# A second rows buffer, one mask tied behind hand-ordered GpSimd work, and a new hand order with dummy matmuls

## The chip, the cores and the metric

The kernel runs on one core of a Trainium2 chip. The metric is device time in microseconds of a whole execution. Names of engines as in the profile: PE is TensorE (PEld its weight loads), DVE is VectorE, ACT is ScalarE, POOL is GpSimd, and SP is the engine whose queue issues nearly all DMAs. Each engine works through its own queue in order, and waits on semaphores for the others.

## The reference

Three layers, one after the other, in float32:

```python
# 1: scan over chunks of 32 positions: x (4, 8, 768, 32), a (4, 8, 768), B and C (4, 8, 768, 16)
log_a = np.log(np.clip(a, 1e-06, 1.0))
for c in range(nc):
    cum = np.cumsum(la, axis=-1)
    L = np.exp(cum[:, :, :, None] - cum[:, :, None, :]) * causal
    M = np.einsum('bhin,bhjn->bhij', Cc, Bc) * L
    y[:, :, sl] = M @ xc + (Cc @ state) * exp(cum)          # written as einsums
    state = exp(sum(la)) * state + sum_j(Bc x xc * exp(cum[-1] - cum))
# 2: x = y as (3072, 256)
h = x @ w_in                      # (256, 2048)
x = np.maximum(0.01 * h, h) @ w_out
# 3: eight experts; each token goes to one
logits = x @ w_gate + modality_bias[modality_id]
e_idx = np.argmax(logits, axis=1)
gate_w = probs[np.arange(N), e_idx]
for e in range(E):
    out[mask] = gate_w[mask, None] * (np.maximum(x[mask] @ w1[e], 0.0) @ w2[e])
```

## The kernel before, in words

**Tiling.** The scan is done in 24 chunks of 128 positions (0 to 23, six for each batch entry). The 3072 tokens form six blocks of 512, four chunks each. Layer 2 takes a block in 16 steps f of 128 hidden units: `mm1` makes `h` (six matmuls 128x512, since operands are split into a high and a low float32r part), ACT and DVE make `sa`, `gg`, `gh`, `gl` from it, and `mm2` adds to two tiles `y` (six matmuls). So a step is twelve matmuls. Layer 3 takes tiles of 256 tokens of one expert; the token lists (`il`) are built on the chip by `ranks`, the rows of x lie in DRAM (`yx`), and a gather brings them back (`xg`).

**Chunks.** A chunk needs `e`, the exponentials of differences of sums, with a mask. For chunks 0 to 3 the sums come from matmuls (`bc_mm`), ACT makes the exponentials (`bc_exp`), and POOL masks them in two halves of 128x512 (`bc_mask`). For chunks 4 and later the sums are broadcast by a DMA from DRAM (`e<-cumd`, 512 KB each, after `cumd<-cumrow` has been written), POOL masks all 128x1024 at once (`attn_mask`), and ACT makes the exponentials behind that (`attn_exp`). Then DVE multiplies (`cb_mul`), PE sums (`p3_mm`, tile `psy`), and ACT and DVE write the chunk's columns of `xh` and `xl`, from which `mm1` reads.

**Weights of layer 2.** They come as 64-bit numbers, 1 MB at a time (`raw`; four for w_in, four for w_out, three buffers), and each half of 128x512 is turned into a high and a low part in five operations: ACT `hb`, POOL `lb` (about 2 us), DVE two operations (the second writes `hb`), ACT `wih` or `woh`, and the subtraction that writes `wil` or `wol`, also on POOL here. The halves called i0, i1 (w_in, first quarter) and o0, o1 (w_out, first quarter) are done in the prologue.

**What sets the order.** The prologue (chunks 0 to 3 and the halves i0, i1, o0, o1) stands in the list `STAGED`, which four engines keep among these entries. All else is placed by a scheduler that simulates the program: the list `sched` says at which of the 16 steps of a block a piece is offered, and numbers in `Q` shift these slots. `sh1` shifts the chunks of block 1 (4 to 7). An operation that is not in `STAGED` may be placed between entries of `STAGED`. SP's queue is ordered by the same scheduler. A DMA on SP waits, among others, for the one eight places ahead of it.

**Rows buffer.** Per block, `route` writes the reciprocal of the softmax sum into the last column of `ysb`, `rows` writes the block's 512 rows into it in two copies, and `rows_out` sends it to `yx`. Before the change there is one `ysb` of 128x1056 for all six blocks.

All operations that the helper class records carry line 153 in the profile, so rows are told apart by tiles.

Of the kernel before, what the change touches and what calls it, by code (L numbers as in the profile page):

```python
# [8 lines left out]
F32 = mybir.dt.float32  # L9
# [5 lines left out]
ALU = mybir.AluOpType  # L15
# [17 lines left out]
 'xe': 2,  # L33
 'se': 8,
 'me': 7,
 'sh1': -2,
 'sh': 0,
 'ld': 9,
 'cd': 4,
# [49 lines left out]
def kernel(  # L89
# [21 lines left out]
    P = 128  # L111
# [140 lines left out]
    def consts_b():  # L252
# [25 lines left out]
        v.memset(base, 0.0)  # L278
        v.memset(wg, 0.0)
        g.memset(ysb, 0.0)  # L280
        nc.sync.dma_start(out=yx[NT:NT + 1, :], in_=ysb[0:1, 0, :])
        nc.sync.dma_start(out=wg[:, :, 0:NE], in_=w_gate.rearrange("(k p) e -> p k e", p=P))
        nc.sync.dma_start(out=modi, in_=mod.bitcast(I32).rearrange("(c p w) -> p c w", p=P, w=2))
        nc.sync.dma_start(out=mb, in_=mbias.unsqueeze(0).to_broadcast([P, 2, NE]))
# [114 lines left out]

    def bc_mm(c, q):  # L400
        b, cc = divmod(c, NCB)
        bc = psy.tile([P, 512], F32, tag="y", name="bc")
        cs = slice(cc * P, (cc + 1) * P)
        if c:
            t_.matmul(bc, lhsT=cumb[:, cs], rhs=negm[:, 4 * q:4 * q + 4].unsqueeze(2).to_broadcast([96, 4, P]), start=True, stop=False)
        for k in range(4):
            r = b * H + 4 * q + k
            o = bc[:, k * P:(k + 1) * P]
            if c:
                t_.matmul(o, lhsT=id3[:, r:r + 1].to_broadcast([96, P]), rhs=cumb[:, cs], start=False, stop=(k == 3))  # L410
# [268 lines left out]
    def route(j, src):  # L679
# [287 lines left out]
    STAGED = [
        (decay_a,), (tr_mm, 0), (bc_mm, 0, 0), (bc_mm, 0, 1), (decay_b,), (tr_c, 0), (tr_b, 0), (decay_rows,),
        (bc_exp, 0, 0), (bc_mask, 0, 0), (bc_exp, 0, 1), (bc_mask, 0, 1), (cb_mm, 0), (decay_high,), (attn_cd, 1),
        (hb, "i0", 0, 0), (lb, "i0"), (decay_low_s,), (cb_bs, 0), (cb_mul, 0, 0), (cb_mul, 0, 1), (decay_low_v,),  # L970
        (cb_mul, 0, 2), (cb_mul, 0, 3), (decay_out,), (tr_mm, 1), (tr_d, 1), (tr_c, 1), (tr_b, 1), (tr_de, 1),
        (bc_mm, 1, 0), (bc_mm, 1, 1), (bc_exp, 1, 0), (bc_mask, 1, 0), (bc_exp, 1, 1), (bc_mask, 1, 1),
        (p3_mm, 0), (orr, "i0"), (p3_x, 0), (p3_st, 0), (decay_full_mm,), (decay_full,), (hb, "i1", 0, 1), (cast, "i0"),
        (attn_cd, 2), (cb_mm, 1), (cb_bs, 1), (cb_mul, 1, 0), (cb_mul, 1, 1), (cb_mul, 1, 2), (cb_mul, 1, 3), (lb, "i1"),
        (tr_mm, 2), (tr_d, 2), (tr_c, 2), (tr_b, 2), (tr_de, 2), (bc_mm, 2, 0), (bc_mm, 2, 1),
        (bc_exp, 2, 0), (bc_mask, 2, 0), (bc_exp, 2, 1), (bc_mask, 2, 1), (p3_mm, 1), (p3_x, 1), (p3_st, 1), (orr, "i1"),
        (sub, "i0"), (cast, "i1"), (attn_cd, 3), (cb_mm, 2), (cb_bs, 2), (cb_mul, 2, 0), (cb_mul, 2, 1), (cb_mul, 2, 2),
        (cb_mul, 2, 3), (tr_mm, 3), (tr_d, 3), (tr_c, 3), (tr_b, 3), (tr_de, 3), (bc_mm, 3, 0), (bc_mm, 3, 1),
        (bc_exp, 3, 0), (bc_mask, 3, 0), (bc_exp, 3, 1), (bc_mask, 3, 1), (p3_mm, 2), (p3_x, 2), (p3_st, 2),
        (sub, "i1"), (hb, "o0", 0, 0), (lb, "o0"), (hb, "o1", 0, 1), (lb, "o1"),  # L980
        (cb_mm, 3), (cb_bs, 3), (cb_mul, 3, 0), (cb_mul, 3, 1), (cb_mul, 3, 2), (cb_mul, 3, 3), (p3_mm, 3), (p3_x, 3), (p3_st, 3),
        (orr, "o0"), (cast, "o0"), (sub, "o0"), (orr, "o1"), (cast, "o1"), (sub, "o1"),
    ]
# [148 lines left out]
```

## Time and profile before

| | |
|---|---|
| median of 3 runs | 561.11 us (558.36 to 562.27) |
| profiled execution, its own time | 560.4 us |
| its span in the trace | 558.3 us |
| PE busy | 508.1 us (91%) |
| DVE, ACT, POOL busy | 351.8 (63%), 312.8 (56%), 194.9 us (35%) |

The sum of the prediction is made against the profiled execution: 558.3 us of span and 2.1 us around it. In the page's second part each digit is the busy share of one fortieth of the span (14 us) in tenths. In lists of instructions a row has the start, the busy time, engine, line, operation, tiles and count, and in brackets how long the engine was idle before it and what ended that. Slices of the second part and the windows show busy time, not progress: a PE that runs at the lower of its two clock levels is also busy.

### The profile page before, as it was taken

The page shows a single profiled execution, that of the slowest core. Times are in us where ns is not written, and L with a number is a line of the kernel's source. Part 1 is how long each engine was busy: PE and PEld are TensorE (multiplying, and loading weights), DVE is VectorE, ACT ScalarE, POOL GpSimd, SP SyncE. Part 2 cuts the span into 40 slices and gives each one's busy share as a digit, 9 for nine tenths or more (in the row PEclk, how much of TensorE's full clock was granted, in tenths as well). Part 3 has the DMA queues.
Part 4 walks back from the last instruction along what each step waited for, and adds up shares of the span by engine and source line. Part 5 has one row for each costly group of instructions (what it writes and reads, how often), then busy time and mean ns, then how long its engine had stood idle before and what let it go on. Part 6 is the DMA issues. An engine that isn't in the chain of part 4 may idle for free.

```text
span 558.3 us, 9625 instructions
## 1 busy us (share of the span) xinstructions
PE 508.1 (91%) x3491; PEld 413.8 (74%) x3491; DVE 351.8 (63%) x729; ACT 312.8 (56%) x651; POOL 194.9 (35%) x167
## 2 busy tenths in 40 slices
PE   7749887899999999999999999698989999999991
PEld 5426555677776777677767777576879999999991
DVE  4738998866656775766576766436486665555640
ACT  5426857774655665565556546244446666665640
POOL 5448788410311020102110020451054364665431
PEclk9868998999999999999999999899999999999996
DMA  8995652330236123523340075626059966777400
GB/s 199 147 256 119 175 157 53 58 59 9 52 51 148 17 52 54 112 46 58 38 107 1 2 61 116 213 72 92 0 171 79 298 212 190 230 240 237 147 20 23
DMA packets 128311, 61.01 MB, mean 109 GB/s; under 512 B 84545, under 2 KB 120514, under 8 KB 128258
## 3 DMA queue, kind: packets, MB, share of 16 engines
q1 hardware_dynamic: 125186, 53.94, 43.4%
q0 software_dynamic: 3072, 6.41, 3.6%
q8 instruction: 29, 0.48, 0.4%
q14 instruction: 24, 0.20, 0.1%
HBM read 53.73 MB, written 6.60 MB: 108 GB/s over the span
## 4 chain that ended last, share of the span: by engine, by line
PE 65%; DVE 10%; issue 6%; DMA 6%; ACT 5%; SPq 3%; POOL 2%; POOLq 0%; DVEq 0%; ACTq 0%
PE h L153 19%; PE y L153 18%; PE hp L153 11%; PE o L153 10%; DMA il<-ids,pi 3%; PE psy L153 3%; DVE gl L153 2%; DVE hb L153 2%; DVE e L153 2%; ACT e L153 2%; DMA yx<-ysb 1%; PE cb L153 1%; SPq L373 1%; DMA e<-cumd 1%; DVE gg L153 1%
## 5 line engine op out<-in xcount | busy, mean ns | idle before, releaser
L153 ACT CAST gh<-gg 128x512 fp32r<-128x512 f32 x96 | 59.5, 620 | 75.8 <-DVE gg L153 75.5
L153 DVE TENSOR_TENSOR gl<-gg,gh 128x512 fp32r<-128x512 f32 x96 | 73.8, 768 | 30.1 <-ACT gh L153 27.9
L153 POOL TENSOR_SCALAR_AFFINE_SELECT e<-e 128x1024 f32<-128x1024 f32 (+1 forms) x28 | 27.4, 985 | 170.2 <-DMA e<-cumd 107.1
L153 PE MATMUL h<-xh,wih 128*128 128x512 f32 x192 | 80.0, 421 | 5.8 <-DVE gg L153 4.9
L153 PE MATMUL y<-gl,woh 128*128 128x512 f32 x192 | 78.0, 406 | 6.5 <-DVE gl L153 6.4
L153 DVE TENSOR_TENSOR gg<-sa,h 128x512 f32<-128x512 f32 x96 | 65.6, 683 | 28.9 <-ACT sa L153 24.5
L153 PE MATMUL h<-xl,wih 128*128 128x512 f32 x192 | 76.9, 401 | 0.0
L153 PE MATMUL y<-gh,wol 128*128 128x512 f32 x192 | 75.8, 395 | 0.0
L153 PE MATMUL h<-xh,wil 128*128 128x512 f32 x192 | 75.7, 397 | 0.0
L153 ACT ACTIVATE sa<-h 128x512 f32<-128x512 f32 x96 | 57.0, 593 | 32.3 <-PE h L153 29.7
L153 PE MATMUL hp<-x2h,w1s 128*128 128x256 f32 x384 | 71.9, 283 | 0.0
L153 PE MATMUL o<-w2s,hh 128*128 128x256 f32 x384 | 69.3, 285 | 0.0
L153 PE MATMUL y<-gh,woh 128*128 128x512 f32 x192 | 66.5, 406 | 2.4 <-ACT gh L153 2.4
L153 DVE SCALAR_TENSOR_TENSOR hl<-hp,hh 128x512 fp32r<-128x512 f32 x48 | 33.0, 691 | 52.7 <-ACT hh L153 38.3
L153 PEld LDWEIGHTS hp<-x2h,w1s 128*128 128x128 f32 x384 | 61.1, 192 | 0.6
L153 POOL TENSOR_TENSOR w2s<-r,w2s 128x1024 fp32r<-128x1024 f32 x12 | 33.1, 2756 | 73.4 <-ACT w2s L153 51.1
L153 PEld LDWEIGHTS o<-w2s,hh 128*128 128x128 f32 x384 | 58.4, 191 | 0.4 <-issue 0.4
L153 PE MATMUL hp<-x2l,w1s 128*128 128x256 f32 x192 | 53.3, 283 | 0.0
L153 PEld LDWEIGHTS h<-xh,wih 128*128 128x128 f32 x192 | 36.6, 193 | 20.2 <-DVE gg L153 9.3
L153 PE MATMUL o<-w2s,hl 128*128 128x256 f32 x192 | 51.1, 283 | 0.0
L153 ACT ACTIVATE e<-e,ncum 128x128 f32<-128x128 f32 x160 | 51.0, 395 | 0.0
L153 ACT ACTIVATE hh<-hp 128x512 fp32r<-128x512 f32 x48 | 28.5, 597 | 39.9 <-PE hp L153 34.0
(191 smaller groups left out, 919.2 us busy)
## 6 DMA issues: line engine op xcount, KB each, us to landing
r<-in_moe_w_dram SPq DMA_DIRECT2D x48, 512.0 KB
e<-cumd SPq DMA_DIRECT2D x20, 512.0 KB
raw<-in_moe_w_in_dram SPq DMA_DIRECT2D x4, 1024.0 KB
raw<-in_moe_w_out_dram SPq DMA_DIRECT2D x4, 1024.0 KB
yx<-ysb SPq DMA_DIRECT2D x6, 528.0 KB
xt<-in_x_dram SPq DMA_DIRECT2D x24, 128.0 KB
ct<-in_C_dram SPq DMA_DIRECT2D x24, 64.0 KB
bt<-in_B_dram SPq DMA_DIRECT2D x24, 64.0 KB
```

Source lines behind the costliest of these rows:

```text
L153: r = f(*args, **kw)
L373: nc.sync.dma_start(out=xt, in_=x[b, :, sl, :].rearrange("h p d -> p h d"))
```

## The change

`ysb` gets a second half, and block j uses half j % 2; the clearing of it covers both. `consts_b` is emitted before the staged list and not behind it. The mask of chunk 4 gets an order dependency (no semaphore) on the last subtraction of the staged list. `warm(c, n)` puts n matmuls of zeros in front of a chunk's `bc_mm`, into the tile that `bc_mm` then overwrites: six ahead of chunk 1's transposes and four ahead of chunk 2's. In `STAGED` the second DVE step of half i1 (`orr`) and `attn_cd` of chunk 3 move ahead of chunk 1's p3, and half o1 is started later. `sh1` goes from -2 to 1, which offers all work on chunks 4 to 7 three steps later.

```diff
- 'sh1': -2,
+ 'sh1': 1,
...
-    ysb = cst.tile([P, 4, YW], F32, name="ysb")
+    ysb = cst.tile([P, 2, 4, YW], F32, name="ysb")
...
     def attn_mask(c):
         e = ch[c]["e"]
         r = g.affine_select(out=e, in_=e, pattern=[[0, H], [1, P]], compare_op=ALU.is_ge, fill=NEG, base=0, channel_multiplier=-1)
+        if c == NC0:
+            tc.add_manual_dep(
+                r.ins, dk["last"].ins.name, mybir.DependencyInfo(mybir.DependencyClass.NoSync, mybir.DependencyReason.DATA),
+                reason="behind the first chunks and conversions in the queue: it waits for a transfer",
+            )
...
     def bc_mm(c, q):
         b, cc = divmod(c, NCB)
-        bc = psy.tile([P, 512], F32, tag="y", name="bc")
+        bc = ch[c].get(("bc", q))
+        if bc is None:
+            bc = psy.tile([P, 512], F32, tag="y", name="bc")
...
-        v.reciprocal(out=ysb[:, 0:nq, DM:DM + 1], in_=sm.unsqueeze(2))
+        v.reciprocal(out=ysb[:, j % 2, 0:nq, DM:DM + 1], in_=sm.unsqueeze(2))
...
-        readers.append(s.copy(out=ysb[:, 2 * qq:2 * qq + 2, 0:DM], in_=yr.rearrange("p (q d) -> p q d", q=2)))
+        readers.append(s.copy(out=ysb[:, j % 2, 2 * qq:2 * qq + 2, 0:DM], in_=yr.rearrange("p (q d) -> p q d", q=2)))
...
-        nc.sync.dma_start(out=yx[t0:t0 + n, :].rearrange("(q p) d -> p q d", p=P), in_=ysb[:, 0:nq, :])
+        nc.sync.dma_start(out=yx[t0:t0 + n, :].rearrange("(q p) d -> p q d", p=P), in_=ysb[:, j % 2, 0:nq, :])
...
+    consts_b()
     cvs = {}
+
+    def warm(c, n):
+        bc = psy.tile([P, 512], F32, tag="y", name="bc")
+        for _ in range(n):
+            t_.matmul(bc, lhsT=zer[:, 0:P], rhs=zer, start=True, stop=True)
+        ch[c]["bc", 0] = bc
...
     def sub(key):
         (r, hi, lo, eng), c = cvs.pop(key)
-        eng.tensor_tensor(out=lo, in0=c[1] if W64 else r, in1=hi.bitcast(F32), op=ALU.subtract)
+        dk["last"] = eng.tensor_tensor(out=lo, in0=c[1] if W64 else r, in1=hi.bitcast(F32), op=ALU.subtract)
...
-        (cb_mul, 0, 2), (cb_mul, 0, 3), (decay_out,), (tr_mm, 1), (tr_d, 1), (tr_c, 1), (tr_b, 1), (tr_de, 1),
+        (cb_mul, 0, 2), (cb_mul, 0, 3), (decay_out,), (warm, 1, 6), (tr_mm, 1), (tr_d, 1), (tr_c, 1), (tr_b, 1), (tr_de, 1),
...
```

**POOL's queue, from the masks of chunk 2 on.** Before, `e_197` and `e_204` are chunks 2 and 3, `e_585`, `e_603`, `e_720`, `e_750` are chunks 4 to 7, `wil` the subtractions of i0 and i1, and `raw_171` holds o0 and o1:

```order
L153 AFFINE_SELECT e_197<-e_197 128x512 x2
L153 TENSOR_TENSOR wil_138<-hb_286,wih_137 128x512
L153 AFFINE_SELECT e_585<-e_585 128x1024
L153 AFFINE_SELECT e_603<-e_603 128x1024
L153 AFFINE_SELECT e_720<-e_720 128x1024
L153 AFFINE_SELECT e_204<-e_204 128x512 x2
L153 TENSOR_TENSOR wil_138<-hb_354,wih_137 128x512
L153 TENSOR_SCALAR lb_489<-raw_171 128x512
L153 TENSOR_SCALAR lb_493<-raw_171 128x512
L153 AFFINE_SELECT e_750<-e_750 128x1024
L153 TENSOR_SCALAR lb_591<-raw_208 128x512
L153 TENSOR_TENSOR wol_140<-hb_488,woh_139 128x512
```

In the changed kernel, from the masks of chunk 3 (`e_204`) on; chunks 4 to 7 are now `e_595`, `e_613`, `e_680`, `e_862`:

```order
L153 AFFINE_SELECT e_204<-e_204 128x512 x2
L153 TENSOR_TENSOR wil_138<-hb_400,wih_137 128x512
L153 TENSOR_SCALAR lb_526<-raw_171 128x512
L153 TENSOR_SCALAR lb_566<-raw_171 128x512
L153 AFFINE_SELECT e_613<-e_613 128x1024
L153 AFFINE_SELECT e_680<-e_680 128x1024
L153 AFFINE_SELECT e_862<-e_862 128x1024
L153 TENSOR_SCALAR lb_601<-raw_208 128x512
L153 TENSOR_TENSOR wol_140<-hb_525,woh_139 128x512
L153 TENSOR_SCALAR lb_619<-raw_208 128x512
L153 TENSOR_TENSOR wol_140<-hb_565,woh_139 128x512
L153 AFFINE_SELECT e_595<-e_595 128x1024
```

Chunk 3's masks, the subtraction of i1 and both `lb` of `raw_171` no longer stand behind any mask of a DMA'd chunk. The masks of chunks 5, 6 and 7 now stand together ahead of the next `lb` and of both `wol`; chunk 4's, the first that block 1 needs, stands behind all of them.

**SP's queue around the broadcasts.** Before:

```order
L371 DMA ct_602<-in_C_dram 128x8x16
L350 DMA cumd_96<-cumrow_245 32x768
L373 DMA xt_582<-in_x_dram 128x8x32
L372 DMA bt_601<-in_B_dram 128x8x16
L371 DMA ct_719<-in_C_dram 128x8x16
L375 DMA e_585<-cumd_96 128x8x128
L375 DMA e_603<-cumd_96 128x8x128
L373 DMA xt_600<-in_x_dram 128x8x32
L375 DMA e_720<-cumd_96 128x8x128
L375 DMA e_750<-cumd_96 128x8x128
L607 DMA raw_580<-in_moe_w_out_dram 128x4x256
```

In the changed kernel:

```order
L350 DMA cumd_96<-cumrow_272 32x768
L371 DMA ct_612<-in_C_dram 128x8x16
L373 DMA xt_592<-in_x_dram 128x8x32
L372 DMA bt_611<-in_B_dram 128x8x16
L371 DMA ct_679<-in_C_dram 128x8x16
L375 DMA e_595<-cumd_96 128x8x128
L614 DMA raw_590<-in_moe_w_out_dram 128x4x256
L375 DMA e_613<-cumd_96 128x8x128
L375 DMA e_680<-cumd_96 128x8x128
L375 DMA e_862<-cumd_96 128x8x128
L373 DMA xt_610<-in_x_dram 128x8x32
```

The write of the sums goes one DMA earlier, and the 1 MB load of w_out's second quarter now stands between the broadcast of chunk 4 and those of chunks 5 to 7.

**ACT's queue in block 0**, in the changed kernel, from the exponentials of chunk 4 to the first operation on step f = 4 (`sa_834`):

```order
L153 ACTIVATE e_595<-e_595,ncum_122 128x128 x7
L153 CAST wih_137<-hb_618 128x512
L153 ACTIVATE e_595<-e_595,ncum_122 128x128
L153 ACTIVATE e_613<-e_613,ncum_122 128x128 x4
L153 ACTIVATE hb_751<-raw_590 128x512
L153 CAST woh_139<-hb_751 128x512
L153 COPY btt_726<-ps_721 128x128
L153 CAST xh_630<-psy_700 128x2x128
L153 ACTIVATE cdt_729<-ps_721,mask2_106 128x128 x2
L153 ACTIVATE e_613<-e_613,ncum_122 128x128 x4
L153 ACTIVATE hb_759<-raw_590 128x512
L153 ACTIVATE sa_834<-h_827 128x512
```

Before, chunk 4's eight exponentials stood ahead of block 0's very first `sa`; now they, and what follows, stand ahead of the `sa` of its fifth step. From the early steps of block 2 to the end the order on every engine is the same in both kernels but for single neighbours.

## Rows read from the trace of the kernel before

**Rows 1.** The page's second part: PE's busy tenths in 40 slices.

```profile
PE   7749887899999999999999999698989999999991
```

**Rows 2.** The chain that ended last, from 0 to 120 us: start, length, what.

```profile
25.76 7.37 issue
33.13 5.65 DMA e<-cumd
...
44.89 4.17 PE h L153 x12
...
103.57 1.66 PE h L153 x6
```

**Rows 3.** Busy time by windows: PE, PEld, DVE, ACT, POOL, clock, DMA share, GB/s.

```profile
30.00:40.00 10.00, 4.16 (x37) 2.30 (x36) 0.97 (x3) 2.18 (x6) 4.42 (x5) 0.67 1.07 283
...
90.00:100.00 10.00, 10.00 (x46) 7.71 (x45) 9.05 (x14) 5.94 (x12) 8.76 (x6) 0.91 0.01 2
...
120.00:140.00 20.00, 20.00 (x111) 15.67 (x108) 12.26 (x29) 11.67 (x29) 1.09 (x1) 1.00 0.20 40
```

**Rows 4.** POOL's instructions in order of time, 20 to 60 us.

```profile
33.17 1.09 POOL L153 TENSOR_SCALAR_AFFINE_SELECT e<-e 128x1024 f32<-128x1024 f32 x1 [7.41 <-DMA e<-cumd]
35.13 1.09 POOL L153 TENSOR_SCALAR_AFFINE_SELECT e<-e 128x1024 f32<-128x1024 f32 x1 [0.87 <-DMA e<-cumd]
37.77 2.27 POOL L153 TENSOR_SCALAR_AFFINE_SELECT e<-e 128x1024 f32<-128x1024 f32 x3 [1.55 <-DMA e<-cumd]
...
47.63 2.00 POOL L153 TENSOR_SCALAR lb<-raw 128x512 int32<-128x512 uint16 x1 [1.41 <-DVE hb L153]
...
53.00 1.30 POOL L153 TENSOR_TENSOR wol<-hb,woh 128x512 fp32r<-128x512 f32 x1
54.94 2.05 POOL L153 TENSOR_SCALAR lb<-raw 128x512 int32<-128x512 uint16 x1 [0.64 <-DVE hb L153]
...
58.88 2.31 POOL L153 TENSOR_SCALAR lb<-raw 128x512 int32<-128x512 uint16 x1 [0.64 <-DVE hb L153]
```

**Rows 5.** ACT's instructions in order of time: the exponentials of chunk 3.

```profile
30.14 1.10 ACT L153 ACTIVATE e<-bc 128x512 f32<-128x512 f32 x2
```

**Rows 6.** SP's DMA issues in order of time, 0 to 70 us.

```profile
24.54 0.81 SPq L371 DMA_DIRECT2D ct<-in_C_dram  x1
...
27.95 1.19 SPq L375 DMA_DIRECT2D e<-cumd  x2
```

**Rows 7.** Windows of 2 us, columns as in group 3.

```profile
34.00:36.00 2.00, 0.16 (x1) 0.00 (x0) 0.00 (x0) 0.00 (x0) 1.13 (x2) 1.00 1.22 257
...
38.00:40.00 2.00, 0.00 (x0) 0.00 (x0) 0.00 (x0) 0.00 (x0) 2.00 (x3) 0.50 1.00 341
```

**Rows 8.** DVE's instructions in order of time, then the chain from 300 to 420 us.

```profile
354.02 0.18 DVE L153 RECIPROCAL ysb<-sm 128x4 f32<-128x4 f32 x1 [6.09 <-DMA yx<-ysb]
...
347.36 6.57 DMA yx<-ysb
```

**Rows 9.** PE's instructions in order of time, 345 to 384 us.

```profile
349.72 0.61 PE L153 MATMUL y<-gh,woh 128*128 128x512 f32 x2
354.32 0.19 PE L153 MATMUL rp<-ohb,tris 128*128 128x32 bf16 x1 [3.99 <-DVE ohb L153]
...
358.73 0.63 PE L153 MATMUL y<-gh,woh 128*128 128x512 f32 x2
...
361.48 0.61 PE L153 MATMUL y<-gh,woh 128*128 128x512 f32 x2
...
375.55 0.60 PE L153 MATMUL xps<-ident,xg 128*128 128x128 f32 x4
```

**Rows 10.** All engines in order of time, 0 to 60 us.

```profile
2.87 0.97 POOL L153 MEMSET ysb<- 128x1056 f32 x1
...
7.64 0.36 DVE L153 COPY cum<-p 128x192 f32<-128x192 f32 x1 [0.90 <-PE p L153]
...
14.22 0.33 PE L153 MATMUL ps<-ident,ct 128*128 128x128 f32 x1 [1.51 <-DVE e L153]
```

More of the change, by code (lines that the diff above doesn't have):

```diff
@@ L280, in consts_b @@
         g.memset(ysb, 0.0)
-        nc.sync.dma_start(out=yx[NT:NT + 1, :], in_=ysb[0:1, 0, :])
+        nc.sync.dma_start(out=yx[NT:NT + 1, :], in_=ysb[0:1, 0, 0, :])
         nc.sync.dma_start(out=wg[:, :, 0:NE], in_=w_gate.rearrange("(k p) e -> p k e", p=P))
@@ L970 @@
         (hb, "i0", 0, 0), (lb, "i0"), (decay_low_s,), (cb_bs, 0), (cb_mul, 0, 0), (cb_mul, 0, 1), (decay_low_v,),
-        (cb_mul, 0, 2), (cb_mul, 0, 3), (decay_out,), (tr_mm, 1), (tr_d, 1), (tr_c, 1), (tr_b, 1), (tr_de, 1),
+        (cb_mul, 0, 2), (cb_mul, 0, 3), (decay_out,), (warm, 1, 6), (tr_mm, 1), (tr_d, 1), (tr_c, 1), (tr_b, 1), (tr_de, 1),
         (bc_mm, 1, 0), (bc_mm, 1, 1), (bc_exp, 1, 0), (bc_mask, 1, 0), (bc_exp, 1, 1), (bc_mask, 1, 1),
-        (p3_mm, 0), (orr, "i0"), (p3_x, 0), (p3_st, 0), (decay_full_mm,), (decay_full,), (hb, "i1", 0, 1), (cast, "i0"),
@@ L974 @@
[L974 to L982, printed above, removed]
+        (p3_mm, 0), (orr, "i0"), (p3_x, 0), (p3_st, 0), (decay_full_mm,), (decay_full,), (cb_mm, 1), (warm, 2, 4),
@@ new lines @@
+        (hb, "i1", 0, 1), (cast, "i0"), (cb_bs, 1), (cb_mul, 1, 0), (cb_mul, 1, 1), (attn_cd, 2), (cb_mul, 1, 2),
+        (cb_mul, 1, 3), (lb, "i1"), (tr_mm, 2), (tr_d, 2), (tr_c, 2), (tr_b, 2), (tr_de, 2), (orr, "i1"), (attn_cd, 3),
+        (bc_mm, 2, 0), (bc_mm, 2, 1), (bc_exp, 2, 0), (bc_mask, 2, 0), (bc_exp, 2, 1), (bc_mask, 2, 1),
+        (p3_mm, 1), (p3_x, 1), (cast, "i1"), (sub, "i0"), (p3_st, 1), (cb_mm, 2), (cb_bs, 2),
+        (cb_mul, 2, 0), (cb_mul, 2, 1), (cb_mul, 2, 2), (cb_mul, 2, 3), (tr_mm, 3), (tr_d, 3), (tr_c, 3), (tr_b, 3), (tr_de, 3),
@@ L983 @@
+        (bc_mm, 3, 0), (bc_mm, 3, 1), (bc_exp, 3, 0), (bc_mask, 3, 0), (bc_exp, 3, 1), (bc_mask, 3, 1),
+        (p3_mm, 2), (p3_x, 2), (p3_st, 2), (sub, "i1"), (hb, "o0", 0, 0), (lb, "o0"), (cb_mm, 3), (cb_bs, 3),
+        (cb_mul, 3, 0), (cb_mul, 3, 1), (cb_mul, 3, 2), (cb_mul, 3, 3), (p3_mm, 3), (p3_x, 3), (orr, "o0"), (p3_st, 3),
+        (cast, "o0"), (hb, "o1", 0, 1), (lb, "o1"), (sub, "o0"), (orr, "o1"), (cast, "o1"), (sub, "o1"),
     ]
@@ L986 @@
             fn(*args)
-    consts_b()
     early = [
```

## The prediction

> **What bounds the kernel now.** First the slices of the page's second part: PE, the engine with most work, falls below nine tenths in the first quarter, around slice 26 and at the end [rows 1]. So three places can give time. Then the chain of waits for the first 120 us: between 25.76 and 38.8 us it is no engine's work at all, but 7.37 us of "issue" and 5.65 us of a broadcast `e<-cumd`; the first `mm1` starts at 44.89 [rows 2]. In the window 30 to 40 us DVE works 0.97 us of 10 while the DMA share is 1.07 [rows 3]. POOL's list shows who stands still: three masks of 128x1024 (chunks 4 to 6) wait 7.41, 0.87 and 1.55 us for their broadcasts, and the row of three at 37.77 is the third of them and then chunk 3's two halves [rows 4]. ACT had chunk 3's exponentials ready from 30.14 on, in two halves, done at 31.24 [rows 5]. Chunk 3 is the last that block 0 needs, so all engines wait for transfers of block 1.
>
> From 45 to about 103 us the bound is DVE and POOL together (9.05 and 8.76 us busy of 10 in 90 to 100), since the weights are converted there; later PE alone is the bound, 20.00 of 20 us, with DVE at 12.26 [rows 3]. The last wait of the chain for DVE's `gg` ends at 103.57 [rows 2].
>
> The second place is at 350 us: DVE stands for 6.09 us before the reciprocal that writes `ysb`, until `yx<-ysb` has landed [rows 8], and PE behind it idles 3.99 us [rows 9].
>
> **The change, part by part.** *Rows buffer.* With two halves the reciprocal of block 4 has to wait for the rows of block 2, not for those of block 3. What the wait cost is read on PE: from one `y<-gh,woh` pair to the next took 349.72 to 358.73 = 9.0 us, the next such step 358.73 to 361.48 = 2.75 us; eight small `rp` matmuls belong to the first (about 0.3). So 9.0 - 2.75 - 0.3 = 5.9 us [rows 9]: the idle time, and slow matmuls after it. DVE's 6.09 us say the same [rows 8]. Nothing else of DVE's is late there: it would be at the reciprocal at 347.9, and `gl` follows. The gathers from `yx` still wait for that transfer (354 us), but PE first reads what they bring at 375.55 [rows 9], 16 us later even when it comes 5.9 us sooner. Ends: 0, if another wait takes its place, and 6.1. I take 5.9.
>
> *Chunk 3 set free.* Chunk 4's mask waits for a DMA and stands first in a queue in which everything else is ready; the change puts it last, and the masks of chunks 5 and 6 go behind the first `lb` pair with it. From the start of chunk 3's masks (37.77 + 1.09 = 38.86) to the first `mm1` at 44.89 are 6.0 us [rows 2, 4]. The masks can now start when ACT's first half is done, 30.14 + 0.55 = 30.7 [rows 5]. First `mm1` at 36.7, 8.2 us earlier.
>
> *What is late next.* POOL's new queue has the masks of chunks 5, 6, 7 ahead of the next `lb` and of both `wol`, and step f = 0 of `mm2` needs the first `wol`. So when does chunk 7's broadcast land? Before, chunk 4's landed at 33.17 and chunk 5's 1.96 us later [rows 4]. The write of the sums now goes one issue earlier, 0.9 us (24.54, 0.81 long) [rows 6]: 32.3. Behind it stands the 1 MB load: at 341 GB/s, the highest of these windows, 3.1 us, at two broadcasts' time 3.9 [rows 4, 7]; I take 3.5, to 35.8. Three broadcasts at 2.0 us: 41.8. Bounds: 38.3 if the 1 MB does not hold them up, 44 if they go at the 257 GB/s of the slowest busy window and share it with the smaller loads [rows 7].
> Rows 4 show broadcasts landing in the order of issue, but none with a large load in front. The Trainium skill ("DMA: Bandwidth & Descriptors", "Queues, rings and completion order") says that each DMA engine takes its descriptors in ring order, though completion is not strictly first in, first out; that speaks against this change, because the load was put ahead of what POOL waits for. By that rule the landing is 41.8 and the head gives 4.6 us; were the load passed by, 38.3 and 8.1.
>
> Mask 7 then ends at 41.8 + 1.1 = 42.9, where POOL's `lb` stood at 47.63: 4.7 us earlier. `lb`, `wol`, `lb`, `wol` take 47.63 to 54.30 = 6.7 us [rows 4], then chunk 4's mask 1.1: the next `lb` at 50.7, not 54.94, 4.2 earlier. The one after it, 3.3 us on, at 54.0, not 58.88, 4.9 earlier, because POOL's two waits of 0.64 us for DVE [rows 4] fall away: DVE has had nothing else to do. So of PE's 8.2 us some 4.6 survive. From there to 103 us both kernels have the same work on the two engines that bind; the lead is carried on, and PE, bound from then on with an unchanged order, carries it to the end. Ends: 0 and 8.2; 4.6 is what POOL's queue gives.
>
> *The rest.* The clearing of `ysb` doubles, 0.97 us more on POOL at 2.9 us; behind it stand small masks that DVE needs before it copies `cum` at 7.64, and DVE is idle 0.90 us there [rows 10]: 0, or 1.0 if that cover fails. Ten dummy matmuls: six fit into PE's idle 1.51 us at 14.22 [rows 10] at 2.75/12 = 0.23 us each [rows 9]; the other four are 0.9 us where PE waits for DVE. I cost them at 0; at twice the pitch and with the first gap alone as cover they cost 10 x 0.46 - 1.5 = 3.1. A higher clock that they may buy for the prologue is worth nothing while POOL is what holds `mm2`. `sh1` moves chunks 4 to 7 three steps later without changing their work: 0, and a rival below. `consts_b` stays where it was in the queues.
>
> Sum: 4.6 + 5.9 = 10.5 us off 560.4, which is 0.7 below the median of 561.1: **549.9 us**.
>
> **The rivals.**
> 1. *As summed*, 549.9, by itself 547 to 553.5 (landing of chunk 7 between 38.3 and 44, and what the dummies may take): chance 0.46.
> 2. *All of PE's lead is kept*: the broadcasts are not held up, and DVE, which idles 9 us in 30 to 40 [rows 3], takes the work of the conversions early. 8.2 + 5.9 = 14.1: 546.3. The rule on ring order named above is against it. Chance 0.16.
> 3. *The lead is lost between 45 and 110 us.* DVE and POOL are near full, chunk 4's mask and exponentials now stand in front of step f = 4, and chunks 4 to 7 press on the end of block 0, so PE waits for `xh` at block 1's start what it won before. For it: the windows show no room on the two engines. Only the rows buffer remains: 554.5. Chance 0.18.
> 4. *The rows buffer gives nothing*: the wait goes over to the next thing that hangs on the same transfer, the gathers, or the halves are tracked as one tile and the change does not do what it says. Against it: they are needed 16 us later. 560.4 - 4.6 = 555.8. Chance 0.12.
> 5. *Slower.* POOL's queue stops at chunk 7's mask instead of chunk 4's, with both `wol`, chunk 4's mask and, through ACT's queue, `sa` of step f = 4 behind it. Each us that its broadcast lands after 41.8 costs a us; from 52.3 on (41.8 + 10.5) the kernel is slower, at 58 it takes 566. Chunk 7's buffer is chunk 1's, and the 1 MB load needs the buffer of halves i0 and i1, so a late conversion would hold SP and all three broadcasts. Against it: POOL was through with chunk 2 and half i0 when its long wait began, at 33.17 - 7.41 = 25.8 [rows 4], and the DMA engines move 257 to 341 GB/s in that stretch [rows 7]. Chance 0.08.
>
> **The numbers.** Predicted is the likeliest, 549.9. Range 544 to 557: down to rival 2 less the 2 us by which runs of this kernel differ, up over rivals 3 and 4; out of it lie rival 5 and single ends, under 0.2. A measurement of this kernel can tell about 1% (5.6 us) from no change, so faster means below 555.5: rivals 1 and 2, most of 3 and a part of 4, 0.77. Within 1%: the rest of 3 and 4 and a small part of 5, 0.16. Slower: 0.07.
>
> **What would show each step.** Right: POOL's masks of chunk 3 near 31 us without a DMA wait ahead of them; a wait for `e<-cumd` on POOL that ends near 42; the first `mm1` at 35 to 37, then a hole on PE until the first `wol` at about 46; PE's last wait for `gg` near 99; no wait of the reciprocal for `yx<-ysb`, and PE's hole at 350 gone. Wrong: chunk 7's mask before 39 or after 46; as many idle us on PE between 45 and 110 as the head won; a new hole on PE between 330 and 400 us.

## The result, and the profile after

The changed kernel takes 552.0 us (median of four runs, 550.48 to 552.88) where the kernel before takes 560.25 beside it: ratio 0.9849, interval 0.9805 to 0.9894. A second series later gave 0.9836 (0.979 to 0.9881). Ratios, here and below, leave out single executions in a slower state of the chip, medians do not, so that a ratio is not always the quotient of the medians beside it. The profiled execution took 550.48 us, with a span of 548.8, 9.5 us less than before. Forecast was 549.9 within 544 to 557. So the total came as forecast, but partly by luck, since it came from other places than the sum said: nearly all of it from the rows buffer, next to nothing from the head.

**The page's slices.** PE's row of the second part, to be held against [rows 1]:

```profile
PE   8857798899999999999999999999989999999991
```

The 6 at slice 26 is gone. The first ten slices have three nines in both kernels, and their digits add up to 78, before to 76: there the busy time mainly stands in other slices.

**The tail.** DVE at the reciprocal of block 4, and PE there, in order of time (after [rows 8, 9]):

```profile
346.69 0.18 DVE L153 RECIPROCAL ysb<-sm 128x4 f32<-128x4 f32 x1
```

```profile
345.83 0.62 PE L153 MATMUL y<-gh,woh 128*128 128x512 f32 x2
...
348.55 0.61 PE L153 MATMUL y<-gh,woh 128*128 128x512 f32 x2
349.00 0.19 PE L153 MATMUL rp<-ohb,tris 128*128 128x32 bf16 x1
...
351.62 0.62 PE L153 MATMUL y<-gh,woh 128*128 128x512 f32 x2
...
368.43 0.60 PE L153 MATMUL xps<-ident,xg 128*128 128x128 f32 x4
```

The reciprocal has no wait in its brackets, and the step with the eight `rp` takes 351.62 - 348.55 = 3.07 us, where it took 9.0. That is the prediction's step, to 0.05 us.

**The head.** POOL's queue in order of time (after [rows 4]):

```profile
31.59 1.22 POOL L153 TENSOR_SCALAR_AFFINE_SELECT e<-e 128x512 f32<-128x512 f32 x2 [5.00 <-ACT e L153]
...
39.16 1.10 POOL L153 TENSOR_SCALAR_AFFINE_SELECT e<-e 128x1024 f32<-128x1024 f32 x1 [1.25 <-DMA e<-cumd]
...
42.87 1.09 POOL L153 TENSOR_SCALAR_AFFINE_SELECT e<-e 128x1024 f32<-128x1024 f32 x1 [0.75 <-DMA e<-cumd]
46.28 1.99 POOL L153 TENSOR_SCALAR lb<-raw 128x512 int32<-128x512 uint16 x1 [2.32 <-DVE hb L153]
...
52.85 1.55 POOL L153 TENSOR_SCALAR_AFFINE_SELECT e<-e 128x1024 f32<-128x1024 f32 x1
55.03 1.97 POOL L153 TENSOR_SCALAR lb<-raw 128x512 int32<-128x512 uint16 x1 [0.63 <-DVE hb L153]
...
58.90 2.33 POOL L153 TENSOR_SCALAR lb<-raw 128x512 int32<-128x512 uint16 x1 [0.64 <-DVE hb L153]
```

Chunk 3's masks are free at 31.59, and chunk 7's broadcast is there at 42.87 (forecast 41.8). But the `lb` that was to follow at 42.9 starts at 46.28, after a wait for DVE, and the two behind chunk 4's mask start at 55.03 and 58.90, where before they started at 54.94 and 58.88 [rows 4]. Of POOL's lead nothing is left at 55 us. PE, DVE and SP's issues show what came in its place:

```profile
38.22 1.22 PE L153 MATMUL h<-xh,wih 128*128 128x512 f32 x2 [0.51 <-ACT xh L153]
45.08 0.80 PE L153 MATMUL h<-xl,wih 128*128 128x512 f32 x1 [5.63 <-DVE xl L153]
```

```profile
44.39 0.29 DVE L153 TENSOR_TENSOR cd<-ct,ecum 128x128 f32<-128x128 f32 x1 [8.12 <-DMA ct<-in_C_dram]
44.60 0.42 DVE L153 TENSOR_TENSOR xl<-psy,xh 128x256 fp32r<-128x256 f32 x1
```

```profile
29.02 0.52 SPq L614 DMA_DIRECT2D raw<-in_moe_w_out_dram  x1
29.60 7.59 SPq L375 DMA_DIRECT2D e<-cumd  x3
...
40.82 1.57 SPq L371 DMA_DIRECT2D ct<-in_C_dram  x1
```

Read from below: three broadcasts keep SP's queue for 7.59 us, and two small loads follow; so chunk 7's `ct` is issued at 40.82 and used at 44.39. On DVE its product `cd` stands one place ahead of chunk 3's `xl`, so DVE stands for 8.12 us, the first `mm1` breaks off after two matmuls, and the conversions that POOL's `lb` needs (`hb`) are late too. One wait for a transfer was moved out of POOL's queue, and another, in DVE's queue, took its place.

The windows say how little that won (after [rows 3], same columns):

```profile
30.00:40.00 10.00, 6.11 (x63) 3.41 (x62) 4.27 (x11) 3.87 (x11) 7.16 (x6) 0.55 1.00 291
40.00:50.00 10.00, 4.92 (x20) 3.52 (x21) 4.75 (x10) 3.44 (x6) 6.17 (x6) 0.60 0.75 117
...
90.00:100.00 10.00, 9.13 (x60) 6.44 (x59) 8.23 (x19) 7.55 (x20) 7.44 (x5) 1.00 0.17 23
...
120.00:140.00 20.00, 20.00 (x128) 15.45 (x128) 13.46 (x35) 11.66 (x29) 1.09 (x1) 1.00 0.16 28
```

DVE does 3.3 us more than before in 30 to 40. In 40 to 50 it does 4.75 us; before it did 8.11 there. By 50 us it has been busy for 27.9 us in all, before for 27.6. In 90 to 100 DVE and POOL have a little more room than before (8.23 and 7.44 us busy, before 9.05 and 8.76), and in 120 to 140 PE is full in both kernels.

**The clearing.** POOL's clearing of `ysb` in the change, and DVE's first work on `a_sb`, before and in the change:

```profile
2.86 1.85 POOL L153 MEMSET ysb<- 128x2112 f32 x1
```

```profile
3.43 0.82 DVE L153 TENSOR_SCALAR a_sb<-a_sb 32x768 f32<-32x768 f32 x1 [0.90 <-DMA a_sb<-in_a_dram]
```

```profile
3.05 2.07 DVE L153 TENSOR_SCALAR a_sb<-a_sb 32x768 f32<-32x768 f32 x1 [0.53 <-DMA a_sb<-in_a_dram]
```

DVE's work ends 0.41 us after the clearing in both kernels, at 4.25 before and at 5.12 in the change. Its copy of `cum` comes 0.87 us later too (8.51, before 7.64), and POOL's first mask 0.84 us (11.83, before 10.99). In e1, e3, e5, e6 and e8 below, `a_sb` is as late, and `cum` comes at 7.81 all the same: there PE is at the higher of its two clock levels by then, in these two only from 9.8 and 10.4 us on.

**A ledger of steps.** Each of the 96 steps of layer 2 has one `gg` on DVE. Their starts, read from DVE's list of every profile, show where time comes and goes. Before: the start in us; the others: difference to it (negative is earlier). Steps 0 to 15 are block 0, 16 begins block 1, 80 block 5; e1 and so on are the runs below, "again" the second profile of the change. How finely such differences may be read is shown by the two profiles of the change: they part by up to 1.1 us in steps 7 to 13, by 0.1 at step 16, and by 2.9 at step 95.

```
step  before   change   again    e1     e11     e2      e3      e4      e5      e6      e8
   0   48.99   -0.75   -0.51   -0.29   -1.10   -3.24   -5.04   -1.14   +1.04   -2.01   -3.40
   3   60.61   -3.77   -3.55   -3.34   -1.36   -6.02   -4.52   -4.17   -0.33   -4.96   -2.36
   4   67.73   +0.40   +0.63   +0.82   +0.78   -1.85   -5.10   +2.20   -0.94   -0.79   -2.92
   8   87.76   -3.07   -2.74   -3.14   -2.35   -5.24   -7.81   -0.21   -2.49   -4.23   -5.12
  11   96.92   -3.02   -1.92   -2.32   -1.48   -5.18   -6.21   +1.95   -2.08   +0.44   -6.41
  12  102.84   +0.18   +1.29   +0.88   -0.18   -1.99   -3.04   +4.16   +1.12   +1.79   -4.85
  15  110.99   +1.90   +2.01   +3.09   +2.38   +0.26   -0.91   +6.72   +3.16   +3.20   -5.93
  16  114.73   +0.14   +0.24   +1.33   +0.89   -1.51   -2.67   +5.28   +1.40   +1.82   +0.53
  40  195.97   -0.31   -0.21   +0.90   -1.20   -1.93   -3.15   +3.08   +1.00   -0.43   -0.91
  81  346.83   -1.15   -0.73   +0.36   -1.77   -2.63   -3.27   +2.88   +0.77   -0.30   -1.22
  82  354.77   -7.12   -6.69   -1.48   -7.73   -8.60   -9.23   -3.08   -5.20   -6.26   -7.18
  88  372.89   -9.56   -9.14   -1.46  -10.17  -11.03  -11.63   -5.53   -6.75   -8.71   -8.83
  95  396.38  -10.79   -7.90   -0.13  -10.28  -12.26  -12.86   -4.41   -2.41   -9.59   -5.18
```

The change is 3 us ahead at step 11 and 0.14 behind at step 16. That is only in part a loss: the two kernels have not done the same work at step 11. Counted in PE's queue, so many steps of `mm1` stand ahead of a chunk's `cb` (first number) and of its sums `psy` (second number):

```
            chunk 4     chunk 5     chunk 6      chunk 7      chunk 8
before      2 / 3       4.8 / 6     7 / 9.7      12 / 15      17 / 19
change      2 / 5.7     6 / 7       11 / 13.7    14 / 15      16 / 18
```

In the change chunk 6 and chunk 7 both fall between steps 11 and 15. On DVE the state of chunk 6 (`st`), in each kernel's list (first before, then after), shows it in time:

```profile
93.02 0.27 DVE L153 TENSOR_TENSOR st<-psy,gm 128x128 f32<-128x128 f32 x1
```

```profile
99.72 0.28 DVE L153 TENSOR_TENSOR st<-psy,gm 128x128 f32<-128x128 f32 x1
...
101.63 0.29 DVE L153 TENSOR_TENSOR bs<-bt,e 128x128 f32<-128x128 f32 x1 [0.59 <-ACT e L153]
102.02 1.08 DVE L153 TENSOR_TENSOR e<-e,cb 128x256 f32<-128x256 f32 x3
103.02 0.68 DVE L153 TENSOR_TENSOR gg<-sa,h 128x512 f32<-128x512 f32 x1
```

Chunk 7's multiplications stand directly ahead of step 12's `gg`. A lead may be read only where the same work is done, and the first such place is step 16, the start of block 1.

At the reciprocal of block 4 (step 82) the difference jumps by 5.97 us, from -1.15 to -7.12. Then, between steps 87 and 95, another 2.8 us come on top (-7.98 at step 87 to -10.79). Layer 3 gives 1.3 back: from step 95 to the end of the span it takes 163.2 us, before 161.9.

### The profile page after: what moved, and what is told of

Read it like the earlier page. It is cut to its first block, busy times and chain, and to the rows that moved or that the text cites. A ratio compares the mean times of both kernels' runs of the same rounds, so it can differ in the third digit from the quotient of the medians.

```text
span 548.8 us, 9656 instructions
## 1 busy us (share of the span) xinstructions
PE 507.1 (92%) x3501; PEld 413.9 (75%) x3501; DVE 350.2 (64%) x729; ACT 312.1 (57%) x651; POOL 196.9 (36%) x167
## 4 chain that ended last, share of the span: by engine, by line
PE 58%; ACT 3%; issue 2%; DVE 2%; POOL 1%; POOLq 0%; DVEq 0%
PE y L153 16%; PE h L153 15%; PE hp L153 12%; PE o L153 10%; PE psy L153 2%; ACT e L153 1%; PE xps L153 1%; PE yr L153 1%; PE ps L153 1%; PE cb L153 1%; POOL out_dram L153 1%; DVE w2s L153 1%; ACT cdt L153 1%; PE lp L153 1%; DVE gg L153 0%
## 5 line engine op out<-in xcount | busy, mean ns | idle before, releaser
L153 POOL TENSOR_SCALAR_AFFINE_SELECT e<-e 128x1024 f32<-128x1024 f32 (+1 forms) x28 | 29.1, 1045 | 171.0 <-DMA e<-cumd 55.9
L153 PE MATMUL y<-gl,woh 128*128 128x512 f32 x192 | 76.7, 402 | 0.7 <-DVE gl L153 0.6
L153 PEld LDWEIGHTS h<-xh,wih 128*128 128x128 f32 x192 | 36.7, 193 | 20.9 <-DVE gg L153 9.1
```

The lines of the kernel that those rows point to most:

```text
L153: r = f(*args, **kw)
```

## The experiments

The kernel before itself had medians of 560.25 to 564.8 us in the series, so that runs are compared by their ratio to it, and places by the profile.

**e1: one half of the rows buffer.** All five engines keep the change's order.

```
-ysb[:, j % 2, ...]
+ysb[:, 0, ...]        # at the reciprocal, the two copies and the store
```

> The changed kernel with one edit: `ysb` keeps its two halves but every block uses half 0, so that block 4's reciprocal again waits for block 3's rows. Nothing else moves: all five engines keep their order. Theory T (the second half is worth what the wait cost, and more): the wait of the reciprocal comes back with about 6 us, and with it the smaller hole of 3 to 4 us at 374 to 380 us, which stands in the profile of before and not in that of the change; 552.0 + 9.6 = 561 to 562 us, nearly the time before. Rival T1: only the 5.9 us of the prediction, 558. Rival T2: the hole at 350 us went for another reason (a shift in time of all that stands ahead of it), 552.

Measured: 561.68 us, 1.0026 of before (0.9983 to 1.0068). DVE's and PE's lists:

```profile
352.53 0.18 DVE L153 RECIPROCAL ysb<-sm 128x4 f32<-128x4 f32 x1 [4.25 <-DMA yx<-ysb]
```

```profile
376.02 0.73 PE L153 MATMUL y<-gh,woh 128*128 128x512 f32 x2 [1.18 <-ACT gh L153]
...
378.58 0.80 PE L153 MATMUL y<-gl,woh 128*128 128x512 f32 x1 [1.83 <-DVE gl L153]
```

Both holes are back, the first with a wait of 4.25 us where before had 6.09, and with them the whole time: theory T. The same run answers the other half of the sum. It has everything of the head, and it isn't faster than before; the forecast 4.6 us would be 0.992, outside its interval.

**e11: the rows buffer alone**, on the kernel before (the lines of the diff that name `ysb`; nothing else).

> The kernel before with the second half of `ysb` alone: no dependency for the mask, `STAGED` and `sh1` as before, no dummies. Theory E (the second half is all that the change brings): 0.983 to 0.987 of before, as the changed kernel. By the prediction's sum (5.9 us of it): 0.9895. If the head part was worth something that the other run hid: 0.99 or more.

Measured: 556.51 us, 0.9864 (0.9819 to 0.9908), 7.6 us of 561 (5.2 to 10.2). Its ledger goes from -1.77 to -7.73 at step 82. The intervals do not part this from the whole change (0.9849). (The longer clearing also makes the scheduler place some work of blocks 0 and later differently; e1, which has no such side effect, says the same.)

**e2: chunk 7's `cd` behind the conversions.** One DVE instruction moves, nothing else.

```
+        if c == NC0 + 3:      # in attn_cd: NoSync dependency on the last hb of the prologue
+            tc.add_manual_dep(r.ins, dk["lastv"].ins.name, ...)
```

> The changed kernel with one DVE instruction moved: chunk 7's `cd`, which waits for its `ct` until 44.39 us, stands behind the last conversion of the prologue instead of ahead of chunk 3's `xl`. Theory A (this wait took the lead that chunk 3 had won): `xl` at about 36.5 instead of 44.60, PE's wait of 5.63 us before 45.08 gone, POOL's third `lb` at about 44 instead of 46.28, the first `gg` near 44.7 instead of 48.24, and 2 to 3.5 us of it are still there at the end: 548.5 to 550. Theory B (the lead is lost later, between steps 8 and 12 of block 0, where it was 3 to 4 us at 90 us and nothing at 103 us): the first steps are 3 us earlier, but step 12's `gg` stays at 103 us and the time at 552, within 1 us.

Measured: 552.3 us, 0.9857 (0.9809 to 0.9905). DVE's list:

```profile
40.07 0.42 DVE L153 TENSOR_TENSOR xl<-psy,xh 128x256 fp32r<-128x256 f32 x1 [1.93 <-ACT xh L153]
...
45.54 0.29 DVE L153 TENSOR_TENSOR cd<-ct,ecum 128x128 f32<-128x128 f32 x1 [0.50 <-DMA ct<-in_C_dram]
45.75 0.68 DVE L153 TENSOR_TENSOR gg<-sa,h 128x512 f32<-128x512 f32 x1
```

The wait is 0.50 us instead of 8.12, PE's 5.63 us are gone, and the first four `gg` come 2.0 to 2.6 us sooner than in the change, although the prologue ran 1.9 us later in this profile (chunk 3's masks at 33.45). So theory A is right on what held the head. Of the gain 1.65 us are left at step 16 and 1.5 at step 81, too little for the times to tell: theory B is right on the total.

**e3: the masks of chunks 4 to 7 behind POOL's prologue as well.**

```
-        if c == NC0:
+        if NC0 <= c < NC0 + 4:   # in attn_mask, with the edit of e2
```

> As the run before, and the masks of chunks 5, 6 and 7 also stand behind the prologue's work on POOL, with that of chunk 4. POOL then runs its four `lb` and two `wol` from 34 to about 43 us without a DMA wait between them, so the first `wol` is there near 40 instead of 49.5. Theory A: steps 0 to 3 another 1 to 4 us earlier, and the total 1 to 2 us under that of the run before, 547 to 549. Theory B: again lost by step 12, 552 within 1 us. Rival C: chunk 4's exponentials, and with them block 1, come later, since all four masks now follow one another behind 44 us: 553 to 556.

Measured: 550.68 us, 0.9831 (0.9773 to 0.9889). POOL's list:

```profile
41.45 1.28 POOL L153 TENSOR_TENSOR wol<-hb,woh 128x512 fp32r<-128x512 f32 x1
...
45.88 5.80 POOL L153 TENSOR_SCALAR_AFFINE_SELECT e<-e 128x1024 f32<-128x1024 f32 x4
```

The first `wol` is there at 41.45 instead of 48.25, and the four masks run without one wait. In the ledger this version leads the kernel before by 3.6 to 8.1 us in steps 0 to 11, by 2.7 at step 16 and by 3.3 at step 81. It is the best of the head versions in the ledger; the interval does not part it from the change.

**e4: `sh1` back at -2.**

```
- 'sh1': 1,
+ 'sh1': -2,
```

> The changed kernel with `sh1` back at -2: the work of chunks 4 to 7 is offered three steps earlier, as in the kernel before. Theory A: chunk 7's `cd` still holds up DVE until 44 us, the lead is small from there on, and the time stays at 552 within 1.5 us. Theory B: the work of chunks 7 and 8 no longer stands ahead of step 12's `gg`; this comes near 100 instead of 103.02 us, and the kernel takes 548.5 to 550. Rival D: the masks and exponentials come before the conversions again and the steps 4 to 8 are later: 553 to 556.

Measured: 556.49 us, 0.9954 (0.9911 to 0.9998). Rival D: it is behind in steps 4 to 7 and from step 9 on, by 5.3 us at step 16. So with the new prologue `sh1` is worth some 5 us, and I had costed it at 0. The rest of the head's edits cost about what it brings: this run, which has them and the rows buffer, is at 0.9954, the rows buffer alone (e11) at 0.9864.

**e5: no dependency for chunk 4's mask.**

```
-        if c == NC0:
+        if c < 0:
```

> The changed kernel without the dependency that ties chunk 4's mask behind the prologue on POOL: this mask stands ahead of chunk 3's two masks again, all other parts of the change are kept. Theory E (the head part is worth nothing on the whole, since what chunk 3 wins is lost again by step 12 of block 0): chunk 3's masks and the first `mm1` come some 2 to 4 us later than in the changed kernel (31.6 and 38.2 us), and the time is 552 within 1.5 us, with the lead at step 40 of the scan of `gg` within 1 us of the changed kernel's. Rival F (the dependency is a real gain, and the other parts of the change, the order and the dummies, cost as much): 555 to 557.

Measured: 557.7 us where before took 564.8, 0.9846 (0.9794 to 0.9897). Its first `mm1` starts at 41.40, 3.2 us later than the change's, and at step 16 it is 1.3 us behind the change. Theory E: the dependency of the mask moves the first steps, and what it does for the whole is too little for the times to tell. (Without it the scheduler also places other work of block 0 differently.)

**e6: dummy matmuls of 8 columns.**

```
-            t_.matmul(bc, lhsT=zer[:, 0:P], rhs=zer, ...)
+            t_.matmul(bc[:, 0:8], lhsT=zer[:, 0:P], rhs=zer[:, 0:8], ...)
```

> The changed kernel with its ten dummy matmuls cut from 512 to 8 columns. If they cost nothing and give nothing (the prediction's 0): 552 within 1 us. If they are what keeps PE's granted clock at 1.00 in 20 to 30 us, where before showed 0.67, and the chain to `mm1` of block 0 hangs on it: 1 to 3 us slower, with the first `mm1` after 39.5 instead of 38.22. If they stand in PE's way: the first `mm1` at 35 to 37 us, and 549 to 551.

Measured: 557.13 us, 0.9846 (0.9792 to 0.9899), the change's ratio. In 20 to 30 us PE's granted clock is 0.72, not 1.00 as in both profiles of the change, and the first `mm1` comes at 37.77, not later than the change's 38.22 and 38.66. But the run does not isolate the dummies: with the shorter matmuls the scheduler places other work differently too (on DVE chunk 7's `cd` stands behind `xl` and one conversion, on SP the broadcasts stand in another order around the 1 MB load). What the clock does is better read from e9, which has the dummies of 512 columns and every queue of the change up to the first expert's `w2s`: its granted clock in 20 to 30 us is 0.66, its first `mm1` comes at 39.69, 1.5 us after the change's, and its first `gg` 0.3 us later. So these dummies do not always bring the higher clock; where it is there, the first `mm1` comes sooner, and little of that is left at the first `gg`. That the dummies are worth 0 on the whole fits these times, but is not shown apart from the rest.

**e7: the change once more.**

> The changed kernel itself once more, so that the runs of this study stand against the same runs of the kernel before: 552 within 1.5 us, 0.985 of before. Both theories expect the same; the span differs from the first profile (548.8) by what the granted clock does in layer 3, up to 2 us.

Measured: 555.31 us where before took 564.8, 0.9836 (0.979 to 0.9881). From step 15 to step 88 its ledger follows the first profile's within 0.7 us; at step 95 it is 2.9 us behind it.

**e8: as e3, with `sh1` = 2.**

> As the run with chunk 7's `cd` and all four masks behind the prologue's work, and `sh1` at 2 instead of 1: the work of chunks 4 to 7 is offered one step later still. Theory B (the chunk work ahead of step 12's `gg` is what eats the lead of 6 us that this version has at step 11): step 12 keeps 1 to 3 us more of it, and the time is 547.5 to 550. Rival G (block 1's first step waits for chunk 7's `xh`, so that what step 12 gains is lost at step 16): the same as there, 550.7 within 1.5 us, or slower.

Measured: 555.22 us, 0.984 (0.9788 to 0.9892). It leads by 5.93 us at step 15 and is 0.53 behind at step 16: rival G. Chunk 7's `cb` and `psy` are then the last work ahead of block 1, and block 1 waits for them. Here later chunk work doesn't save time; it moves the wait to the next place where it is needed.

**e9: the first expert's `w2s` on DVE alone.**

```
-split(..., v if k == 0 else g)
+split(..., v if k == 0 or i == 0 else g)   # in m2_split2
```

> The changed kernel with one operation given to another engine: the second half of the first expert's `w2s` (2.41 us on POOL, behind its fourteen DMA issues of 355 to 374 us) is subtracted on DVE, like the first half. Theory H (the hole that PE has at 374 to 380 us in before, and that is there or not in the other runs, comes from this operation: while POOL does it, DVE's `gl` of 128x512 takes 2.53 to 3.20 us, else 0.69): no `gl` over 1 us between 360 and 385, no wait of PE over 1 us there, and 0 to 2 us less than the changed kernel, 550 to 552 or 0.981 to 0.985 of before. Rival J (DVE's 1.25 us more stand in front of `gl` where ACT's `w2s` already delays `gh`): the same hole of 2 to 3 us, 0.985 to 0.989.

Measured: 551.69 us where before took 564.4, 0.9766 (0.9729 to 0.9803). Its profiled execution (556.41) is the longest of its six. No `gl` takes over 1 us in 360 to 385, as theory H has it. PE has a hole all the same, for another reason; ACT's and PE's lists:

```profile
374.39 0.60 ACT L153 ACTIVATE sa<-h 128x512 f32<-128x512 f32 x1 [4.19 <-remote]
```

```profile
375.76 0.80 PE L153 MATMUL h<-xh,wih 128*128 128x512 f32 x1 [2.73 <-DVE gg L153]
```

**e10: e3 and e9 together.**

> Both moves that gave something in the ledger of `gg` together: chunk 7's `cd` and the masks of chunks 4 to 7 behind the prologue's work, and the second half of the first expert's `w2s` on DVE. By the ledger (2.8 us at step 16 against the changed kernel, and 0 to 2 at steps 87 to 91): 548 to 550, or 0.977 to 0.981 of before. If what is won ahead of layer 3 is given back there (in the run with both moved, layer 3 took 166.2 us from the last `gg` to the end, against 163.2 in the first profile of the change): 551, 0.983.

Measured: 553.06 us, 0.9762 (0.9713 to 0.9811).

**e12: the rows buffer and e9's move on the kernel before.**

> The kernel before with two edits of the tail and none of the head: the second half of `ysb`, and the second half of the first expert's `w2s` on DVE instead of POOL. If the head part of the change is worth nothing (theory E) and the move of `w2s` is worth the 0.8% that it showed on top of the change (0.9766 against 0.9836 to 0.9849): 0.974 to 0.982 of before, as the change with that move. If the head part helps where the tail no longer holds: 0.984 to 0.987, as with the second half alone.

Measured: 552.05 us where before took 561.4, 0.9859 (0.9793 to 0.9924), with the shortest span of all profiles, 546.0. It doesn't repeat what e9 and e10 showed. That e9 and e10 beat the change by 0.7 to 0.9% is what their series says; whether the move of `w2s` does it stays open. Layer 3 is where it may lie: from step 95 to the end e9 and e12 take 160.0 us and e10 162.0, all other profiles 161.9 to 166.2. But the move also makes the scheduler place layer 3's work differently on PE, DVE and ACT, and no run parts the two. By its expectation 0.9859 would mean that the head helps once `w2s` is moved. Against this, e9's ledger at step 81 is at -0.20, e12's at -1.47: no lead of the head shows there. The intervals of e9 and e12 overlap (0.9803 and 0.9793), and this too stays open.

## Why the prediction was right, and where it was not

**Rows buffer.** The step was right to its size: 5.97 us at step 82 in the ledger, forecast 5.9, and PE read what the gathers brought at 368.43 without a wait. The term was mis-sized all the same, since the sum stopped at that step. Between the times of e1 and the change lie 1.8% (1.0026 against 0.9849), some 10 us; on the kernel before it is 7.6 us (5.2 to 10.2, so 5.9 alone would fit that one). In the ledger the rest comes 20 us later. Before, POOL's `w2s` and DVE's `gl`, and PE behind them, stood so (DVE, POOL and PE, from three lists):

```profile
377.44 2.53 DVE L153 TENSOR_TENSOR gl<-gg,gh 128x512 fp32r<-128x512 f32 x1 [0.23 <-ACT gh L153]
```

```profile
376.97 2.45 POOL L153 TENSOR_TENSOR w2s<-r,w2s 128x1024 fp32r<-128x1024 f32 x1 [3.62 <-ACT w2s L153]
```

```profile
377.46 0.73 PE L153 MATMUL y<-gh,woh 128*128 128x512 f32 x2 [1.31 <-ACT gh L153]
380.02 0.50 PE L153 MATMUL y<-gl,woh 128*128 128x512 f32 x1 [1.83 <-DVE gl L153]
```

and in the change, DVE and POOL:

```profile
373.84 3.20 DVE L153 TENSOR_TENSOR gl<-gg,gh 128x512 fp32r<-128x512 f32 x1 [0.69 <-ACT gh L153]
```

```profile
374.06 2.41 POOL L153 TENSOR_TENSOR w2s<-r,w2s 128x1024 fp32r<-128x1024 f32 x1
```

Before, ACT's conversion of `w2s` delays `gh` (1.31 us) and POOL's delays `gl` (1.83 us) in one step, 3.1 us of PE. POOL's `w2s` stands behind its fourteen DMA issues, which start when the rows have landed (355.11 before, 355.27 after), so POOL did not move while PE's steps came 7 us earlier. Before, POOL was through with them at 373.35 and waited 3.62 us for ACT's `w2s`; in the change it was through at 374.05, when ACT's had long been done. So in the change the two delays fall on different steps, three apart, and PE has other matmuls in hand for each: no wait there.

Why ACT's `w2s` came so late before is another matter. ACT before, then in the change:

```profile
372.25 0.60 ACT L153 ACTIVATE sa<-h 128x512 f32<-128x512 f32 x1 [2.32 <-remote]
374.41 0.59 ACT L153 COPY ysb<-yr 128x512 f32<-128x512 f32 x1 [1.56 <-PE y L153]
374.89 1.99 ACT L153 CAST w2s<-r 128x1024 fp32r<-128x1024 f32 x2
```

```profile
362.70 0.60 ACT L153 ACTIVATE sa<-h 128x512 f32<-128x512 f32 x1 [0.75 <-PE h L153]
363.59 0.59 ACT L153 COPY ysb<-yr 128x512 f32<-128x512 f32 x1 [0.29 <-PE yr L153]
364.08 2.00 ACT L153 CAST w2s<-r 128x1024 fp32r<-128x1024 f32 x2
```

This is step 88 in both. Before, PE had done its `h` at 369.80 and its `yr` at 370.69, and ACT stood all the same; e1 has the same two waits (3.03 and 1.57 us). They are longer together than the 1.31 us that PE then waited for `gh`, and 1.6 of the 2.8 us of the ledger come in at this step (-7.98 to -9.56). So the two `w2s` are what PE waits behind, but that the second buffer takes these waits of ACT away is not shown. The prediction named the gathers as fixed by that transfer and asked only what PE reads of them; it did not ask what else stands behind them in POOL's queue.

This second gain isn't safe. Of the twelve profiles with two halves, six show no wait of PE over 1 us there (the change, e2, e3, e6, e11, e12), e4 and e7 one of 1.4 and 1.05 us for `gl`, and e5, e8, e9 and e10 one of 2.1 to 3.6 us that ends at 372 to 377 us, together with a wait of ACT of 2.2 to 4.2 us that the profile puts down to "remote". The records don't show what these waits of ACT are, and it stays open.

**Chunk 3 set free.** Right as far as it went: masks at 31.59 (30.7 forecast), first `mm1` at 38.22 (36.7). About 0.9 us of both is the longer clearing, whose cover failed (see below).

**What is late next.** This is the step that failed: "DVE has had nothing else to do". It took POOL's queue as the only one with a wait in it. The landing of chunk 7 was right to 1.1 us (42.87 against 41.8, by broadcasts that queue behind the 1 MB load; 38.3 had the load been passed by). That row agrees with the Trainium skill's rule ("DMA: Bandwidth & Descriptors", "Queues, rings and completion order") that each DMA engine takes its descriptors in ring order. But the same load and the same three broadcasts also hold SP, and with it `ct`, and DVE's queue has chunk 7's `cd` ahead of chunk 3's `xl`. Before, that `cd` ran at 44.82, when everything waited for POOL's masks anyway; the cover was the very wait that the change removes. The `lb` forecast at 50.7 came at 55.03, 4.3 us later: 1.06 since chunk 7's mask ended at 43.96, not 42.9; 2.32 for DVE's `hb`; 0.45 since chunk 4's mask took 1.55 us, not 1.1; 0.63 for the wait for DVE that was to fall away; and 0.13 less for the steps between.

**"The lead is carried on."** This failed as well, and not only for want of a lead. e3 makes one, of 3.6 to 8.1 us, and 2.7 us of it reach step 16. The steps of block 0 take what chunks 4 to 7 leave them. e4 and e8 show both sides: chunk work offered sooner holds steps 4 to 7, offered later it holds step 16. Rival 3 is what happened in the head (554.5 for the whole); the rows buffer then gave what it lacked. The forecast total was right by luck: a term of 4.6 that is about 0 and a term of 5.9 that came out at 7.6 to 10 offset each other.

**The rest.** Clearing at 0: wrong by 0.87 us at the start, the case that the prediction gave as "1.0 if that cover fails". It looked for what waits behind the clearing on POOL; the loss is DVE's first work on `a_sb` beside it, 2.07 us where before it took 0.82. All thirteen profiles with the longer clearing have this work at 1.76 to 2.10 us, and it ends at 5.12 or 5.13 in each. Dummies at 0: not contradicted (e6), not shown either. `sh1` at 0: wrong by about 5 us in this prologue (e4); the total doesn't show it, as the other edits of the head cost about as much.

## What to carry to other kernels

When a wait is taken out of one engine's queue, go through the queues of all engines for the next instruction that waits for a transfer, and through the DMA queue for when that transfer is issued: here what the old wait had hidden became the new one. Read a lead only where both kernels have done the same work (here at a block's start), not at the first step that comes sooner. And a change that bundles edits should be run in parts: here one part of it, the second rows buffer, holds all the gain that the times can tell.

## What the runs showed of the hardware

- **DVE beside POOL.** `gl` (two inputs, 128x512) takes 0.69 us alone and 2.53, 2.52 and 3.20 us beside POOL's `w2s` of 2.4 us, and ends 0.55 to 0.57 us after it in the two profiles shown. The Trainium skill ("SBUF — State Buffer", "SBUF: two separate sides") says that a DVE operation with two SBUF inputs and a GpSimd operation that reads SBUF exclude each other for the whole instruction. The ends in these rows agree; which of the two had started first they do not settle (in the change `gl`'s row begins at 373.84, `w2s`'s at 374.06). With `w2s` off POOL (e9) no `gl` there takes over 1 us. DVE's first work on `a_sb`, with one input, shows the like beside POOL's clearing: it ends 0.41 us after it, whether the clearing takes 0.97 or 1.85 us.
- **Issue is not free for broadcasts.** Three broadcasts of 512 KB kept SP's queue for 7.59 us behind a 1 MB load; before, with no such load ahead of them, the first two took 1.19 us [rows 6] and two more 3.53. The small loads behind them are issued that much later. No run moves the load alone, so that it is the cause is argued and not shown.
- **One order of PE's queue, two granted clocks.** With the same queue up to the first expert, ten dummies of 512 columns included, PE is granted 1.00 in 20 to 30 us in both profiles of the change, the higher of its two levels throughout, and 0.66 in e9, a mean of the two levels. Before, without dummies, it is 0.67. The first `mm1` comes at 38.22, 38.66 and 39.69 in the three; the first `gg` at 48.24, 48.48 and 48.52.
